# Moving the values' part, one VectorE sum and the last unit's products in a hand-ordered HGRN2 and MLP kernel

## The chip, the core and the metric

The kernel runs on one core of one Trainium2 chip. The metric is the device time of one execution in microseconds. TensorE, VectorE (DVE), ScalarE (ACT), GpSimd (POOL) and the queue of SyncE (SP) each work through a list of instructions of their own and wait for one another by semaphores.

## The reference

A gated linear attention with a state of 48 x 48 for each head is followed by a two-layer MLP with the quick GELU. All is float32.

```python
def _attn_ref(q, k, v, f_logit):            # (4, 8, 768, 48)
    f = 1.0 / (1.0 + np.exp(-f_logit))
    for t in range(S):
        state = f[:, :, t, :, None] * state + np.einsum('bhd,bhe->bhde', k[:, :, t], v[:, :, t])
        y[:, :, t] = np.einsum('bhd,bhde->bhe', q[:, :, t], state)

def _moe_ref(x, w_in, w_out):               # x: 3072 tokens x 384, d_ff 2048
    h = x @ w_in
    g = h * (1.0 / (1.0 + np.exp(-1.702 * h)))
    return g @ w_out
```

Between the two, y is brought from (batch, head, token, 48) to x with one row of 384 for each token.

## The kernel before

**Units and stages.** The 3072 tokens are cut into 12 units of 256. For each unit there is an attention part and an MLP part. The MLP of earlier units is used as filler: `fill` is a list of small jobs (columns of work, a function that emits them), and `merge(n, ...)` emits the attention of unit n part by part, each followed by so many jobs of `fill` as its share of the columns allows. For units 4 and up the shares are the numbers that `late(kind)` returns. TensorE and GpSimd keep the order in which the program emits their instructions. The orders of VectorE, ScalarE and SP are made by the scheduler of the framework from the same program.

**The attention of a late unit.** Its parts, in order, are: two parts "V" and one "V3", each of which makes the scores of two levels of a tree over the tokens (L406), multiplies the gates into X (`promote`, L492, VectorE), sets keys and queries aside (`set_aside`, L463 and L469, ScalarE) and masks the scores into A; "C" and "C2", in which the keys are transposed on VectorE, written to memory and fetched again (`carry_k` and `fetch_k`: L558, L563, L572), and copied to `kn` by ScalarE (L573); "B" and "B2", which transpose the gates and queries of the next unit; "S1", the values' part: `add` multiplies the values with A into the bank tile `y` (L503), and the keys `kn` with the values (L594), after which VectorE updates the state `st` (L609 to L613) and GpSimd multiplies gates together (`tot`, L397); "K3", the next keys. The products of the state with the queries (L634) are emitted with the first "V" of the next unit. Their result is copied to yT (L646), moved by DMA to xT (L669, L674), and summed to the operands E on GpSimd (`sums_of_x`, L879). In unit 11, the last, keys are turned on TensorE ("T"), and "S" and "W" close the attention.

**The MLP of a late unit.** h is made of 20 products of sums of w_in with sums of x instead of 24 (`mlp_h20`). An output out of 0 to 7 is a sum of several products, named in `PRODUCTS`: operands, the product on whose PSUM bank it goes on (its parent), and the outputs with signs.

```python
        ("c1", "q0", -1, ((0, -1),)), ("p1", "v", 2, ((6, -1),)), ("a21", "w", -1, ((5, -1),)), ("p3", "r3", 4, ((0, -1),)),
        ("c4", "w", 9, ((2, 1), (0, -1))), ("p9", "x", 7, ((1, -1),)), ("a20", "q0", 19, ((4, -1),)),
        ("p11", "y", 3, ((1, -1),)), ("p12", "b00", 10, ((2, 1),)), ("a30", "t", 18, ()), ("p14", "b01", 17, ((3, 1),)),
```

A product that goes on in its parent's bank must come after every reader of that bank; where a parent has two children, ScalarE copies the bank to another (L923). The first part of an output is copied to g by ScalarE (L935), the later ones are added by VectorE (L939), and when the last has come ScalarE takes the GELU in place (L941). c4 is the one product with two outputs: out 2 is copied from its bank, and its part of out 0 is then added from the copy in SBUF. The order of the products and the bank ("lane") of each stand in `WHOLE`; lanes 0 to 3 are four single banks, 4 and 5 the tile `y`, 6 and 7 the tile `sc`. The last unit has 258 columns and so does each product in two halves, of which the order is `HALVES` (a number of 20 and more is the second half). Then `sums_of_a` makes S from g (L720 to L724), and `mlp_o7` makes the output of 7 products of 8 matmuls each (L785), in the order Y, W, X, Y, Z, Y, Z, with `last_sum` (L729) after X; `lanes["o"]` gives their banks. In the last unit `sum_last` (L964, L966) sums one more token on VectorE.

Of the kernel before, what the change touches and what calls it, by code (L numbers as in the profile page):

```python
# [9 lines left out]
F32 = mybir.dt.float32  # L10
# [3 lines left out]
ALU = mybir.AluOpType  # L14
# [9 lines left out]
def kernel(  # L24
# [33 lines left out]
    nc = tc.nc  # L58
    B, H, S, D = q.shape
    DM = H * D  # L60
    DFF = moe_w_in.shape[1]
    P = 128
    C = 64
    G = 128
    U = 256
# [7 lines left out]
    NK = DM // P  # L73
# [15 lines left out]
    mlp = ctx.enter_context(tc.tile_pool(name="mlp", bufs=2))  # L89
# [13 lines left out]
    def bank(shape, name, lane=None):  # L103

        lane = next(turns) % 4 if lane is None else lane
        return ps.tile(shape, F32, tag=f"mm{lane}", name=name, bufs=1)
# [33 lines left out]
    at = [wp.tile([P, n], I32, tag="bits", name=f"at{j}", bufs=PAIRS_AHEAD) for j, n in enumerate((1, (NL - 1) * 64))]  # L140
# [35 lines left out]
    for r in range(NGR):  # L176
        ffs = range(r * FG, (r + 1) * FG)
        for ff in ffs[::2]:
            f = slice(ff * P, (ff + 2) * P)
# [132 lines left out]
    def attention(n):  # L312
# [304 lines left out]
        def _():  # L617
# [44 lines left out]
            if n > N_FILL:  # L662
                sums_of_x(n)
# [19 lines left out]
    HF, HC = NFF // 2, DM // 2  # L683
    T = {}
# [46 lines left out]
    def mlp_o7(n, g):  # L731
# [74 lines left out]
    WHOLE = tuple((x, 0, lane) for x, lane in (  # L806
        (18, 0), (0, 2), (7, 1), (2, 3), (17, 4), (15, 2), (9, 1), (13, 0), (19, 5), (1, 3),
        (14, 4), (4, 2), (10, 5), (6, 3), (8, 1), (3, 2), (5, 0), (16, 3), (12, 5), (11, 2),
    ))
    HALVES = tuple((x % 20, x // 20, lane) for x, lane in (  # L810
        (38, 7), (20, 1), (22, 2), (7, 0), (37, 7), (35, 1), (2, 6), (27, 3), (9, 0), (34, 5),
        (33, 4), (1, 6), (21, 2), (8, 0), (39, 7), (29, 3), (24, 4), (26, 2), (18, 5), (6, 6),
        (30, 7), (36, 2), (13, 0), (16, 6), (32, 7), (17, 5), (25, 1), (28, 3), (0, 7), (5, 2),
        (19, 6), (4, 0), (23, 4), (10, 6), (15, 7), (3, 0), (14, 5), (12, 6), (31, 4), (11, 0),
    ))
    lanes = {}
    WA = {f"a{i}{c}": w_in[:, c, ROW[i] * FG * P:(ROW[i] + 1) * FG * P] for i in range(ROWS) for c in range(NK)}
# [47 lines left out]
    def sums_of_x(n):  # L865

        w = (width(n) + 1) // 2
        sums = [mlp.tile([P, NK, width(n)], F32, tag="xT", name=f"E_{n}_{i}", bufs=3).rearrange("p c t -> p (c t)")
                for i in range(2)]
        at = iter([sums[i][:, j * w:(j + 1) * w] for i in range(2) for j in range(2 * NK)])  # L870
        e = E[n] = {f"b{c}{j}": xTs[n][:, c, j * w:(j + 1) * w] for c in range(NK) for j in range(2)}
        for out, x, op, y in (
            ("s7", "b11", "", "b21"), ("u", "b20", "", "b21"), ("z", "b01", "", "u"), ("q0", "z", "", "b00"),
            ("v", "u", "+", "b11"), ("w", "b10", "", "v"), ("t", "b01", "+", "b21"), ("x", "b00", "", "w"),
            ("q4", "q0", "+", "b10"), ("r3", "b00", "", "b10"), ("r3", "r3", "+", "b20"), ("y", "x", "", "b01"),
        ):
            if out not in e:
                e[out] = next(at)
            nc.gpsimd.tensor_tensor(e[out], e[x], e[y], ALU.add if op else ALU.subtract)  # L879
# [1 line left out]
    E = {}  # L881
    in_y = {}

    def mlp_h20(n, g):
        w = (width(n) + 1) // 2
        groups = 1 if FG * w <= 512 else 2
        wide = FG // groups
        plan = WHOLE if groups == 1 else HALVES
        lane_of = {(x, group): lane for x, group, lane in plan}
        left = {}  # L890
        for x, group, _ in plan:
            for out, _ in PRODUCTS[x][3]:
                left[out, group] = left.get((out, group), 0) + 1
        single = {key for key, times in left.items() if times == 1}
        begun, banks, shared = set(), {}, {}
        in_y[n] = len(plan)

        def take(lane, name):
            if lane < 4:
                banks[lane] = bank([P, wide, w], f"h_{n}_{name}", lanes["h"][lane])  # L900
            else:
                tag = "y" if lane < 6 else "sc"
                if tag not in shared:
                    shared[tag] = ps.tile([P, 2, 512], F32, tag=tag, name=f"h_{n}_{tag}")
                banks[lane] = shared[tag][:, lane % 2, :wide * w].rearrange("p (t x) -> p t x", x=w)
            return banks[lane]

        def product(x, group, lane):
            a, b, parent, parts = PRODUCTS[x]
            root = parent < 0  # L910
            ph = take(lane, f"{x}_{group}") if root else banks[lane]
            kids = [y for y in range(len(PRODUCTS)) if PRODUCTS[y][2] == x]
            goes_on = any(lane_of[y, group] == lane for y in kids)
            for t in range(wide):
                f = group * wide + t
                nc.tensor.matmul(  # L916
                    ph[:, t], lhsT=WA[a][:, f * P:(f + 1) * P], rhs=E[n][b], start=(root and t == 0), stop=not goes_on,
                    skip_group_check=True,
                )
            in_y[n] -= 1  # L920
            for y in kids:
                if lane_of[y, group] != lane:
                    nc.scalar.copy(take(lane_of[y, group], f"{y}_{group}"), ph)  # L923
            part, turned = ph, 1
            for out, sign in parts:
                key = out, group
                f = ROW[out // 2] * FG + group * wide
                to = g[f // HF][:, f % HF:f % HF + wide, out % 2 * w:(out % 2 + 1) * w]
                left[key] -= 1
                if key in single:  # L930
                    nc.scalar.activation(to, ph, AF.Gelu_apprx_sigmoid, scale=float(sign))
                    continue
                if key not in begun:
                    begun.add(key)
                    nc.scalar.activation(to, ph, AF.Copy, scale=float(sign))  # L935

                    part, turned = to, sign
                    continue
                nc.vector.tensor_tensor(to, to, part, ALU.add if sign == turned else ALU.subtract)  # L939
                if not left[key]:  # L940
                    nc.scalar.activation(to, to, AF.Gelu_apprx_sigmoid)  # L941

        def begin():
            for half in range(2):
                g[half] = g_tile(f"g_{n}_{half}", width(n))
            free = lanes["o"]

            lanes["h"] = [free[x] for x in (1, 2, 0, 3)]
            lanes["o"] = [lanes["h"][x] for x in (1, 0, 3, 2)]

        def end():
            sums_of_a(n, g)
            if width(n) > U:
                sum_last(g)

        return [(0, begin, 0)] + [(wide * w, lambda x=x: product(*x), 0) for x in plan] + [(0, end, 0)]

    def sum_last(g):

# [12 lines left out]
    def width(n):  # L972

        return U + 2 * (n == NALL - 1)

    def g_tile(name, w=U):
        return mlp.tile([P, HF, w], F32, tag="g", name=name, bufs=3)
# [39 lines left out]
        for lo, hi in ((1, 113), (113, P)) if r0 < 0 else ((0, P),):  # L1017
            nc.sync.dma_start(out=out[r0 + lo:r0 + hi, :], in_=o[lo:hi])

    def mlp_unit(n):  # L1020
        g = {}

        def last_token():
            po = ps.tile([P, DM], F32, tag="sc", name="o_last")
            nc.tensor.matmul(po[:1], lhsT=ones, rhs=g["last"][:, 0], start=True, stop=True)
            nc.scalar.copy(g["last"][:1, 0], po[:1])
            nc.sync.dma_start(out=out[NALL * U - 1:, :], in_=g["last"][:1, 0])
        o = mlp_o7(n, g)
        if width(n) > U:
            o.insert(6 * HF, (DM, last_token, 0))  # L1030
        if n > N_FILL:
            return mlp_h20(n, g) + o
        by_block = {}

        def end():

            g[0], g[1] = (by_block["tile", i] for i in range(2))
            sums_of_a(n, g)
            sums_in_place(nc.gpsimd)
            lanes["o"] = [next(turns) % 4 for _ in range(4)]  # L1040
        return mlp_h(n, range(NFF), by_block) + [(0, end, 0)] + o[:HF] + [(0, lambda: sums_in_place(nc.vector), 0)] + o[HF:]

    sums = {}
# [113 lines left out]

    def late(kind):

        return {"V": 7, "V3": 3, "C": 2, "C2": 4, "S1": 3, "S": 7, "B": 3, "B2": 4, "K3": 3, "T": 2, "W": 5}.get(kind, 0)  # L1160

    UNIT = NFF * NK * U + U // P * NFF * DM
    H20 = 20 * FG * G
# [16 lines left out]
    fill = []  # L1180
# [7 lines left out]
    merge(3, fill, 3 * UNIT // 2 - LAG // 2, steady, 7, by=0.7, chores=w_sums, per=1)  # L1188
    fill_order.close()
    for n in range(N_FILL, NALL):  # L1190
        fill += mlp_unit(n)
    with nc.allow_non_contiguous_dma("one token"):
        for h in range(2):
            nc.sync.dma_start(out=q_end[h * HS:h * HS + D], in_=q[B - 1, h::2, S - 1, :].rearrange("a d -> d a"))
# [6 lines left out]
    for n in range(4, NALL):  # L1201
        merge(n, fill, (H20 if n > N_FILL + 1 else NFF * NK * U) + 7 * HF * HC, late, chores=w_sums if n == 4 else [])
# [31 lines left out]
```

## Time and profile before

| what | before |
| --- | --- |
| median of 3 runs (lowest to highest) | 626.68 us (626.68 to 627.51) |
| the profiled execution: time, span | 629.15 us, 627.4 us |
| mean granted TensorE clock | 0.989 |
| TensorE matmuls, 7824 | 586.6 us busy (93%) |
| TensorE weight loads | 519.4 us (83%) |
| VectorE, ScalarE, GpSimd | 433.3 us (69%), 293.0 us (47%), 135.8 us (22%) |
| chain of work that ended last: TensorE, VectorE, ScalarE, DMA | 68%, 15%, 7%, 4% |
| start of L594 in units 5 to 10 | 285.95, 331.85, 377.53, 423.45, 469.17, 514.21 us |
| last unit: first product of h, first matmul of o, end | 579.94, 602.99, 627.4 us |

A row of the trace gives the start in us from the beginning of the span, the duration, the engine (PE matmul, PEld weight load, DVE, ACT, POOL, SPq for a DMA issue), the line and the tiles; "x16" says that 16 instructions stand in one row; one float32 matmul shows as two. In brackets stands how long the engine had been idle and what released it.

### The profile page before, as it was taken

The numbers are of one execution on the slowest core, as the hardware profiler recorded it, in microseconds if no ns is written. First come the engines' busy times: TensorE is split into PE (matmuls) and PEld (weight loads), VectorE is DVE, ScalarE is ACT, GpSimd is POOL, SyncE is SP. The second block draws the span as 40 slices with busy tenths as digits, with TensorE's granted clock in tenths as the row PEclk, the third lists the DMA queues.
The fourth block names the chain that finished last, engine by engine and source line by source line (L and its number), as shares of the span: only waits on it lengthen the run. The fifth ranks groups of instructions, "written<-read, shape, count | busy, mean of one in ns | idle before, by whom it ended". The sixth has DMA issues, their size and how long they took to land.

```text
span 627.4 us, 18499 instructions
## 1 busy us (share of the span) xinstructions
PE 586.6 (93%) x7824; PEld 519.4 (83%) x7824; DVE 433.3 (69%) x693; ACT 293.0 (47%) x611; POOL 135.8 (22%) x215
## 2 busy tenths in 40 slices
PE   6869899889999999999999999989989999999896
PEld 5656776657768689898998999989989989989886
DVE  1799966665887677689577689677687685461293
ACT  3466633343325354365365374474464464542530
POOL 3020200230035405501502501502502404203000
PEclk9979999979999999999999999999999999999999
DMA  7746756741044543433543243443251111001000
GB/s 172 203 121 168 186 137 168 167 125 51 2 104 94 139 114 78 107 83 102 138 105 74 72 111 73 126 124 76 74 150 40 44 53 27 26 2 39 14 1 27
DMA packets 83317, 58.31 MB, mean 93 GB/s; under 512 B 33634, under 2 KB 75266, under 8 KB 83234
## 3 DMA queue, kind: packets, MB, share of 16 engines
q1 hardware_dynamic: 82480, 55.94, 35.7%
q10 hardware_dynamic: 753, 1.18, 0.8%
q8 instruction: 62, 1.02, 0.7%
q14 instruction: 22, 0.17, 0.1%
HBM read 43.98 MB, written 8.39 MB: 83 GB/s over the span
## 4 chain that ended last, share of the span: by engine, by line
PE 68%; DVE 15%; ACT 7%; DMA 4%; issue 3%; SPq 1%; POOL 1%; DVEq 0%; ACTq 0%; POOLq 0%
PE h L916 11%; PE o_Y L785 10%; PE h L993 9%; PE o L1007 8%; PE o_Z L785 7%; PE sc L406 6%; PE h_y L916 4%; PE o_X L785 4%; PE o_W L785 3%; DVE g L939 2%; ACT g L941 2%; ACT kn L573 2%; PE t L350 2%; PE y L634 1%; PE sc L594 1%
## 5 line engine op out<-in xcount | busy, mean ns | idle before, releaser
L492 DVE TENSOR_TENSOR X<-X,tot 128x1024 f32<-128x1024 f32 x45 | 57.7, 1282 | 65.2 <-PE sc L406 55.2
L993 PE MATMUL h<-xT,w_in 128*128 128x256 f32 x384 | 89.3, 388 | 1.1 <-issue 0.7
L463 ACT COPY Kc<-X 128x512 f32<-128x512 f32 x72 | 48.1, 668 | 86.6 <-DVE X L492 59.7
L993 PEld LDWEIGHTS h<-xT,w_in 128*128 128x128 f32 x384 | 73.0, 193 | 13.2 <-issue 1.1
L1007 PE MATMUL o<-w_out,g 128*128 128x384 f32 x192 | 68.1, 504 | 2.4 <-DVE w_out L228 2.0
L397 POOL TENSOR_TENSOR tot<-F 128x512 f32<-128x512 f32 x12 | 12.5, 1040 | 245.3 <-DVE st L612 239.1
L916 PE MATMUL h<-E,w_in 128*128 128x128 f32 (+1 forms) x428 | 56.8, 277 | 3.2 <-DVE g L939 3.2
L1007 PEld LDWEIGHTS o<-w_out,g 128*128 128x128 f32 x192 | 36.5, 195 | 25.9 <-DVE w_out L228 2.6
L916 PEld LDWEIGHTS h<-E,w_in 128*128 128x128 f32 x428 | 51.7, 192 | 4.3 <-issue 3.9
L785 PE MATMUL o_Y<-T,S 128*128 128x192 f32 x288 | 51.7, 329 | 1.1 <-ACT osb L759 1.1
L941 ACT ACTIVATE g<-g 128x512 f32<-128x512 f32 (+1 forms) x63 | 35.9, 584 | 28.2 <-DVE g L939 28.0
L997 ACT ACTIVATE g<-h 128x256 f32<-128x256 f32 x64 | 24.0, 382 | 52.9 <-PE h L993 52.5
L785 PEld LDWEIGHTS o_Y<-T,S 128*128 128x128 f32 x288 | 47.1, 190 | 1.9 <-ACT osb L759 1.4
L456 DVE COPY_PREDICATED A<-masks,sc 128x256 f32<-128x256 uint32 x96 | 42.2, 510 | 0.0
L646 ACT COPY yT<-y 48x256 f32<-48x256 f32 x96 | 35.1, 365 | 11.0 <-PE y L634 9.8
L406 PE MATMUL sc<-X,Kc 48*64 48x64 f32 x1440 | 31.4, 224 | 7.8 <-DVE A L435 3.4
L406 PEld LDWEIGHTS sc<-X,Kc 48*64 48x64 f32 x1440 | 26.6, 138 | 14.5 <-ACT Kc L463 7.8
L338 DVE STREAM_TRANSPOSE X<-raw 128x512 f32<-128x512 f32 x36 | 38.1, 1106 | 0.2
L939 DVE TENSOR_TENSOR g<-g,h 128x512 f32<-128x512 f32 (+1 forms) x49 | 31.5, 647 | 8.3 <-PE h L916 7.2
L935 ACT ACTIVATE g<-h 128x512 f32<-128x512 f32 (+1 forms) x52 | 28.0, 554 | 17.0 <-PE h L916 16.0
L365 POOL TENSOR_SCALAR F<-F 128x1024 f32<-128x1024 f32 x11 | 13.4, 1217 | 102.1 <-ACT F L368 79.1
L879 POOL TENSOR_TENSOR E<-xT 128x128 f32<-128x128 f32 (+1 forms) x32 | 19.0, 603 | 69.9 <-DMA xT<-yT 42.1
(150 smaller groups left out, 1163.2 us busy)
## 6 DMA issues: line engine op xcount, KB each, us to landing
bits<-in_moe_w_out_dram SPq DMA_DIRECT2D x8, 768.0 KB, 8.0
raw<-in_f_logit_dram SPq DMA_DIRECT2D x48, 96.0 KB, 2.4
raw<-in_k_dram SPq DMA_DIRECT2D x48, 96.0 KB, 2.3
raw<-in_q_dram SPq DMA_DIRECT2D x44, 96.0 KB, 2.3
bits<-in_moe_w_in_dram SPq DMA_DIRECT2D x7, 576.0 KB
k_tok<-z SPq DMA_DIRECT2D x56, 64.0 KB, 1.7
kt<-k_tok SPq DMA_DIRECT2D x14, 256.0 KB, 2.8
xT<-yT SPq DMA_DIRECT2D x24, 144.0 KB, 2.7
```

What stands on the lines that cost most here:

```text
L338: nc.vector.transpose(view(out, at, [[HALF, NP], [step, R4], [R4 * step, 32]]), by_half[:, j, f].rearrange("p a (j d) -> p (a j) d", j=R4) ...
L406: nc.tensor.matmul(t["sc"][g * HS:(g + 1) * HS, h, a, s, :], lhsT=t["Kc", l][rows(h), x:x + HS], rhs=rhs(h, a, g), start=True, stop=True,)
L456: nc.vector.copy_predicated(out=view(A, at, dims), mask=mask.bitcast(U32), data=got)
L463: nc.scalar.copy(c.rearrange("p (n two m) -> p n two m", two=2, m=m), view(X, KF * SLOT, [[2 * m, SLOT // (2 * m)], [(KR - KF) * SLOT + m, ...
L492: nc.vector.tensor_tensor(x, x, y, ALU.mult)
L646: nc.scalar.copy(view(yT[rows(h)], at, [[U, NP], [step, HS]]), py[columns(h, g), g, :, f, :])
L785: nc.tensor.matmul(t[name], lhsT=lhs(f), rhs=rhs(f), start=(new and i == 0), stop=(i == HF - 1), skip_group_check=True,)
L916: nc.tensor.matmul(ph[:, t], lhsT=WA[a][:, f * P:(f + 1) * P], rhs=E[n][b], start=(root and t == 0), stop=not goes_on, skip_group_check=True,)
L939: nc.vector.tensor_tensor(to, to, part, ALU.add if sign == turned else ALU.subtract)
L941: nc.scalar.activation(to, to, AF.Gelu_apprx_sigmoid)
L993: nc.tensor.matmul(ph, lhsT=w_in[:, c, ff * P:(ff + 1) * P], rhs=xTs[n][:, c, :], start=(c == 0), stop=(c == NK - 1))
L1007: nc.tensor.matmul(t["po"], lhsT=g[ff // FG][:, ff % FG, tt * P:(tt + 1) * P], rhs=w_out[:, ff, :], start=(ff == ffs[0]), stop=(ff == ffs[ ...
```

## The change

Five edits, none of which adds or removes a matmul, a sum or a transfer.

1. `late` has new shares: V 6 for 7, S1 2 for 3, B 4 for 3, B2 5 for 4, K3 2 for 3. In the built program of each of units 5 to 10 the second scores come 2 o matmuls earlier, the third scores 2 products earlier, and L503 and L594 come 6 o matmuls later (after 8 of Y instead of 2). In unit 11 L634 comes after 4 matmuls of Y instead of 6.
2. In `mlp_h20` a part of an output that lies in SBUF is put off until the next part of that output has been added from its bank.
3. `HALVES` has another order and other lanes, and four marks (-1, -1).
4. The last 16 jobs of `fill`, the last two products of o of unit 10, are taken out of it and emitted in fours at the marks, among the first five half products of unit 11.
5. `sums_of_x` of the last unit makes the sums in another order: t, the seventh, comes fifth; y comes last as before, x ahead of it.

GpSimd's four sums of w_in in unit 4 come ahead of the gates' products (L397) as a result of edit 1.

```diff
+    HALVES = tuple((x % 20 if x >= 0 else None, x // 20, lane) for x, lane in (
+        (38, 1), (-1, -1), (0, 6), (37, 4), (-1, -1), (-1, -1), (39, 4), (-1, -1), (34, 5), (2, 7),
+        (15, 6), (30, 4), (33, 1), (22, 0), (18, 3), (1, 7), (20, 2), (25, 5), (32, 4), (24, 1),
+        (6, 7), (35, 2), (13, 6), (17, 3), (21, 0), (23, 1), (16, 7), (4, 5), (7, 2), (19, 4),
+        (26, 0), (27, 7), (5, 6), (14, 3), (10, 4), (9, 2), (29, 7), (3, 5), (36, 0), (31, 1),
+        (12, 4), (8, 2), (28, 7), (11, 5),
     ))
...
+        if width(n) > U:
+            sums = [sums[i] for i in (0, 1, 2, 3, 6, 4, 5, 8, 9, 10, 7, 11)]
...
-                nc.vector.tensor_tensor(to, to, part, ALU.add if sign == turned else ALU.subtract)
+                if part is not ph and left[key]:
+                    later[key] = part, sign * turned
+                    continue
+                for part, sign in ((part, sign * turned), *filter(None, [later.pop(key, None)])):
+                    nc.vector.tensor_tensor(to, to, part, ALU.add if sign > 0 else ALU.subtract)
...
-        return [(0, begin, 0)] + [(wide * w, lambda x=x: product(*x), 0) for x in plan] + [(0, end, 0)]
+        items = [(0, begin, 0)]
+        for x in order:
+            if x[0] is None:
+                items += before[:4]
+                del before[:4]
+            else:
+                items.append((wide * w, lambda x=x: product(*x), 0))
+        assert not before
+        return items + [(0, end, 0)]
...
+        if width(n) > U:
+            before = fill[-2 * HF:]
+            del fill[-2 * HF:]
...
-        return {"V": 7, "V3": 3, "C": 2, "C2": 4, "S1": 3, "S": 7, "B": 3, "B2": 4, "K3": 3, "T": 2, "W": 5}.get(kind, 0)
+        return {"V": 6, "V3": 3, "C": 2, "C2": 4, "S1": 2, "S": 7, "B": 4, "B2": 5, "K3": 2, "T": 2, "W": 5}.get(kind, 0)
```

## The prediction

> **What bounds the kernel now.** I read the busy table first, then the waits, then two stretches by time. TensorE's order is written out by hand, so every wait of TensorE moves all that stands behind it. The summary line and the waits of its weight loads (columns: us in total, times, longest):
>
> ```profile
> PE 586.6 (93%) x7824; PEld 519.4 (83%) x7824; DVE 433.3 (69%) x693; ACT 293.0 (47%) x611; POOL 135.8 (22%) x215
> ```
>
> ```profile
> PEld sc L594 <- ACT kn L573: 7.3, 7, 1.3
> ...
> PEld h L916 <- issue: 3.9, 4, 1.4
> ...
> PEld y L503 <- DVE g L939: 3.5, 5, 1.4
> ```
>
> No other engine is near full, yet TensorE waits in each late unit for two things: the turned keys `kn`, and a PSUM bank that VectorE has not yet read. By time, the end of the products in the stage of unit 9 (columns: start, us, engine, line; idle before and its releaser in brackets):
>
> ```profile
> 463.56 0.69 DVE L939 TENSOR_TENSOR g<-g 128x512 f32<-128x512 f32 x1 [0.79 <-ACT g L935]
> 464.36 0.69 DVE L939 TENSOR_TENSOR g<-g,h 128x512 f32<-128x512 f32 x1
> ...
> 465.19 1.13 PE L916 MATMUL h<-E,w_in 128*128 128x128 f32 x8 [0.66 <-DVE g L939]
> ...
> 466.16 0.82 PE L785 MATMUL o_Y<-w_out,g 128*128 128x192 f32 x4
> ...
> 466.28 1.83 ACT L941 ACTIVATE g<-g 128x512 f32<-128x512 f32 x3 [0.57 <-DVE g L939]
> ...
> 466.90 1.11 PE L503 MATMUL y<-A,vt 64*48 64x64 f32 x64
> ...
> 468.01 1.10 ACT L573 COPY kn<-kt 128x512 f32<-128x512 f32 x1
> ...
> 469.17 1.03 PE L594 MATMUL sc<-vt,kn 64*64 64x48 f32 x56 [1.15 <-ACT kn L573]
> ```
>
> The reader is to see two stalls. The sum `g<-g` reads SBUF only, waits for ScalarE, and stands in front of the sum that frees the bank of p3; product p11 on that bank comes late. Then `kn` is copied behind three GELUs, and the values' products (L594) wait for it, since two o matmuls alone stand between the products and the values' part. In units 6 and 8 the first stall falls on L503 instead (1.4 us: it needs the bank of p12). The last stage, by busy time (us; busy of PE, PEld, DVE, ACT, POOL), and one of its waits:
>
> ```profile
> 580.00:603.00 23.00, 20.15 (x162) 18.55 (x161) 9.34 (x23) 12.62 (x34) 0.00 (x0) 1.00 0.03 10
> ...
> 584.44 0.61 PE L916 MATMUL h_y<-xT,w_in 128*128 128x129 f32 x4
> 585.16 0.42 DVE L939 TENSOR_TENSOR g<-g,h_y 128x258 f32<-128x258 f32 x1 [4.50 <-PE h_y L916]
> ...
> 585.64 0.52 PEld L916 LDWEIGHTS h_y<-E,w_in 128*128 128x128 f32 x4 [0.78 <-DVE g L939]
> ```
>
> Here each of the 40 half products waits for its bank's last reader: eight waits in a stage in which no engine is full.
>
> **What the Trainium skill says.** "Perfetto Trace Analysis", section Identifying the Most-Contended Engine: matmul busy time is a poor measure of headroom, weight-load busy a better one. The trace agrees: in the last stage PE shows 20.15 of 23.00 us, though a half product with no wait starts every 0.445 us (586.08, 586.52, 586.97), so 40 need 17.8. The same page, Optimization Strategy, advises interleaving stages with different limits; no run yet shows what that is worth here. Its section Optimizing Tensor Performance has independent matmul groups rotate over banks so that evacuations overlap: the old order returns to a bank after as little as three to four products. "PSUM — Partial Sum Buffer", section Engine vs sequencer instructions: the queues of ScalarE, VectorE and GpSimd are strict FIFO. The trace agrees: the second kt transfer is issued at 462.24, lands 2.8 us later, and its copy runs at 468.01, behind the GELUs.
>
> **The change part by part.** No matmul, sum or transfer is added or removed; all five edits move work. Where they move it I took from the order of the built programs.
>
> *1. Pacing (`late`).* In the stages of units 5 to 10 the values' part (L503, L594) comes after eight o_Y matmuls instead of two: 6 x 0.328 us (o_W: 2.60 us for 8) = 1.97 us more cover. Removed wait: `kn`, 7 x about 1.0 = 7.3 us. TensorE would come to L594 at 466.90 + 1.0 + 1.97 = 469.9 in unit 9, against `kn` ready at 469.1; ScalarE's order also puts that copy ahead of one or two GELUs in most units. The same cover takes the two 1.4 us waits of L503, 2.8. If it failed, `kn` would have to be 1.97 us later than now. Of L503's five waits I leave the three of 0.23.
>
> *2. The SBUF sum behind the bank's sum.* p3's sum no longer waits for ScalarE: it can start when VectorE is free at 462.8 instead of 464.36, so p11 loses its wait: 3.9 us over four stages. In even units VectorE has an attention product (L492) ahead of that sum; I leave 0.2 us three times, 0.6. Bounds for edits 1 and 2 together: 9 to 14.0 us gained.
>
> *3. What is late next.* With six o matmuls fewer behind L594, the chain of the attention shows: states (8 x 0.39), `tot` on GpSimd (1.04), F's transposes (2.06), tanh, the yT copies (3.01), Kc, L492, Kc, then the second scores. From the end of L594 to the second Kc is ready it now takes 13.6 us (470.24 to 483.8; even: 424.53 to 438.3), of which 0.25 to 0.7 is VectorE finishing the sums of g, which will be done earlier: 13.1 to 13.3. TensorE's own way to the second scores will be 12 o (3.93) + L634 (0.93) + the first scores (1.2) + 20 o (6.55) = 12.6 us. Now it is 15.4, which leaves the margin seen here:
>
> ```profile
> 483.17 0.62 ACT L463 COPY Kc<-X 128x512 f32<-128x512 f32 x1 [1.07 <-DVE X L492]
> ...
> 485.61 0.69 PE L406 MATMUL sc<-Qc,Kc 48*64 48x64 f32 x32
> ```
>
> So a new wait of 0.5 to 0.9 us; I take 0.7 in six units, 4.2 us. (At unit 4 a like wait, 1.4 us on o_Y after L844, is there already and I leave it.) Bounds: 0 (if the chain loses its VectorE part and the 0.6 us shuffle of values) to 1.5 each, 9 us. The third scores come 1.8 us earlier among the products, but from the second scores to the fourth Kc copy it takes 6.1 us and TensorE has 7.3 of work: covered. L634 follows L594 by 3.93 us, the states need 3.2: covered by 0.7.
>
> *4. Queues passed.* DVE, ACT and SP are in a scheduler's order: a shuffle of values (0.58) moves ahead of L492 in one unit, the key transposes move ahead of sums of g, vr and raw loads change places on SP. SP is idle from 470.8 to 479.2 in unit 9, so I cost these at nothing; without that gap an xT transfer would be up to 4 us late, against E sums that are ready some 4 us before their use. In unit 4 four GpSimd sums of w_in (about 1.26 each) move ahead of the gates' products; GpSimd is idle there until 241.87, so nothing.
>
> *5. Unit 11.* Four o_Y instead of two stand behind L634, which waits for the states in any case: 2 x 0.33 = 0.7 us lost.
>
> *6. The last h.* 16 o matmuls of unit 10 (5.2 us) now stand in four groups among the first five half products, the least return to a bank rises from 1.3-1.8 us to 2.2 us, and a bank's turn takes 0.72 (matmul to reader) + 0.42 + 0.06 = 1.2 us plus queueing. Stage now: 579.94 to 602.99 = 23.05 us, needed 17.8, so 5.2 is lost; I take 4.8 as regained. The E sums on GpSimd are the risk of the earlier start: by the rows of now s7 (first) is done at 574.5, q0 (fourth) at 575.9 and t, now fifth, at 576.4; with edit 5 the products that read them come at about 575.6, 577.3 and 577.8. Bounds 2 to 5.2. VectorE's end work (sum_last 15 x 0.62) ends at 616.2, 2.6 us before it is read at 618.80: it covers one or two of those sums being later.
>
> Sum: -7.3 - 2.8 - 3.9 + 0.6 + 4.2 + 0.7 - 4.8 = **-13.3 us**. On the profiled execution that is 627.4 to 614.1 of span (its own time 629.15). The median of the runs shown, 626.68, lies 2.5 below that time, so I subtract from the median: **613.4**.
>
> **Rivals.** (a) *No new wait*: the attention chain shortens as much as TensorE's way. For it: VectorE starts the states later than it must today. Against: GpSimd, ScalarE and VectorE rows of it are fixed. -13.3 - 4.2 = -17.5: 609. (b) *The cover is half spent*: the second scores wait 1.5 us in six units (+4.8) and the last stage keeps 2 us more of its waits: -6.5: 620. For it: ScalarE and VectorE queue in bursts (three GELUs in a row). (c) *Slower*: the second scores (L406) become the bound of every late unit. Without that wait the change gains 17.5, so it turns slower where the wait exceeds 17.5 / 6 = 2.9 us, a chain of 15.5 us or more after L594; at 3.5 us the sum is +3.5: 630. Against: the longest now is 13.8. (d) *It doesn't do what it says*: the moves cover waits that come back at the next product, and the time stays at 626 to 627. Against: the order of TensorE does change in every late unit and the waits have 1.97 us to hide 1.3.
>
> **How the numbers follow.** Forecast 0.60 (610 to 617), (a) 0.12, (b) 0.17, (c) 0.07, (d) 0.04. The range 607.5 to 621 takes in the forecast, (a) and (b). A measurement can tell 0.2%, 1.3 us, from no change. Faster 0.89, same 0.04, slower 0.07.
>
> **What would show it.** Right: L594's wait for `kn` is gone or under 0.3; p11 and L503 show no wait for g beyond 0.2; a wait L406 <- Kc or X of 0.5 to 0.9 stands before the second scores; from the first last-unit product to the first o_Y of that unit 23 to 24 us pass with the 16 o matmuls inside. Wrong: a wait over 1.5 us at L406, L634 or an early half product, or late units still 45.7 to 45.9 us apart (I expect 44.1).

## The result, and the profile after

The changed kernel takes 622.95 us (median of 20 runs, 619.80 to 627.41) against 626.87 us before (20 runs, 625.47 to 630.63): the ratio of the means is 0.9947, 95% interval 0.9926 to 0.9967, and the medians lie 3.9 us apart. The forecast was 13.3 us less. The profiled execution has a time of 625.44 us, a span of 623.5 us and a mean clock of 0.985.

The waits of TensorE's weight loads in the late units, 238 to 552 us of the changed kernel (total, times, longest):

```profile
PEld sc L406 <- ACT osb L762: 9.6, 6, 2.9
PEld h_y L922 <- DVE g L950: 2.0, 5, 0.6
...
PEld y L503 <- DVE S L720: 0.9, 4, 0.2
PEld y L503 <- DVE g L722: 0.5, 2, 0.2
```

The wait for `kn` at L594 (7.3 us before), the wait of p11 (3.9) and the long waits of L503 are gone, as forecast. In their place stand 9.6 us at L406, the second scores. The end of the products in the stage of unit 9, by time:

```profile
462.20 0.68 DVE L950 TENSOR_TENSOR g<-g,h 128x512 f32<-128x512 f32 x1
...
462.83 2.77 PE L785 MATMUL o_Y<-w_out,g 128*128 128x192 f32 x16
...
463.45 1.13 ACT L573 COPY kn<-kt 128x512 f32<-128x512 f32 x1
...
465.52 1.11 PE L503 MATMUL y<-A,vt 64*48 64x64 f32 x64
...
466.46 1.10 PE L594 MATMUL sc<-vt,kn 64*64 64x48 f32 x64
```

Eight o matmuls now cover the copy of `kn`, which is done at 464.58, 1.9 us before it is used. So edits 1 and 2 do what they say. Fifteen microseconds later come the second scores of the next unit, unit 10:

```profile
477.56 2.76 PE L785 MATMUL o_Z<-T,g 128*128 128x192 f32 x16
...
480.04 1.29 DVE L456 COPY_PREDICATED A<-masks,sc 128x256 f32<-128x256 uint32 x2
480.15 0.62 ACT L463 COPY Kc<-X 128x512 f32<-128x512 f32 x1 [1.08 <-DVE X L492]
...
481.44 0.59 PEld L406 LDWEIGHTS sc<-Qc,Kc 48*64 48x64 f32 x32 [1.41 <-ACT osb L762]
481.47 0.70 PE L406 MATMUL sc<-Qc,Kc 48*64 48x64 f32 x32 [1.15 <-DVE A L456]
```

The second scores start at 481.47. Kc is ready at 480.77, but L456, with which VectorE reads the first scores out of the tile `sc`, ends at 481.33. The weight load's row names an older ScalarE copy, the matmul's row names the one that ended last. The last stage, from the first half product to the first o_Y, with the 16 o matmuls in it, and its waits:

```profile
573.48:600.98 27.50, 24.92 (x194) 23.59 (x194) 9.79 (x24) 11.95 (x33) 1.06 (x3) 1.00 0.04 16
```

```profile
PEld h_sc L922 <- DVE g L950: 1.1, 1, 1.1
PEld h_sc L922 <- ACT g L941: 0.9, 2, 0.7
PEld h_y L922 <- ACT g L937: 0.7, 1, 0.7
PEld h_sc L922 <- ACT h_sc L929: 0.6, 1, 0.6
PEld h_y L922 <- DVE g L950: 0.6, 2, 0.3
```

Before, 23.05 us and 5.2 us for the same o matmuls make 28.25. So 0.75 us was gained where 4.8 was forecast: seven waits, 3.9 us together, are left, all of them on lanes 4 to 7. And the clock: stretches of 2.5 us of the changed kernel after the new wait of unit 5, and after L634 in unit 11 (busy time of PE, PEld, DVE, ACT and POOL, then the granted clock, DMA share and GB/s):

```profile
252.50:255.00 2.50, 0.66 (x5) 0.37 (x3) 1.77 (x3) 1.43 (x4) 0.00 (x0) 1.00 0.42 96
255.00:257.50 2.50, 1.69 (x67) 1.66 (x68) 1.06 (x3) 0.55 (x3) 1.66 (x4) 0.95 0.64 160
257.50:260.00 2.50, 2.50 (x10) 2.50 (x9) 2.50 (x6) 1.14 (x2) 2.42 (x5) 0.50 0.66 134
260.00:262.50 2.50, 2.50 (x15) 2.50 (x14) 1.71 (x3) 0.62 (x1) 2.42 (x5) 0.87 0.20 37
...
555.00:557.50 2.50, 1.14 (x43) 0.79 (x45) 2.33 (x7) 0.00 (x0) 0.00 (x0) 1.00 0.00 0
557.50:560.00 2.50, 2.50 (x47) 2.35 (x48) 0.59 (x2) 1.52 (x5) 0.00 (x0) 0.53 0.02 7
560.00:562.50 2.50, 2.50 (x10) 2.50 (x9) 0.00 (x0) 2.03 (x7) 0.00 (x0) 0.50 0.33 70
562.50:565.00 2.50, 2.50 (x11) 2.50 (x10) 0.00 (x0) 0.00 (x0) 0.00 (x0) 0.61 0.40 87
```

By the clock record of the trace, of which these are means, the clock stands at half for 3.4 us in unit 5 and for 6.8 us in unit 11, and matmuls there take up to nearly twice as long: in unit 11, 4 matmuls of o_Y and 8 of o_W together take 2.75 us more than elsewhere. Before, the clock at the same place of unit 11 stayed full:

```profile
560.00:562.50 2.50, 1.78 (x45) 1.19 (x47) 2.33 (x7) 0.00 (x0) 0.00 (x0) 1.00 0.00 0
562.50:565.00 2.50, 2.28 (x52) 2.15 (x53) 0.61 (x2) 1.76 (x5) 0.00 (x0) 1.00 0.02 7
```

Adding up the profiled executions: from L594 of unit 4 to L594 of unit 11 the kernel gained 4.9 us (319.21 to 314.32), forecast 9.2. From there to the start of the last o_Z it lost 2.9 (62.11 to 65.00), forecast a gain of 4.1. What is left of the 3.9 us of span is the last store, which took 4.6 us from its issue to the end before and 2.8 after and has nothing to do with the change.

### The profile page after: what moved, and what is told of

Read it like the earlier page. It is cut to its first block, busy times and chain, and to the rows that moved or that the text cites. A ratio compares the mean times of both kernels' runs of the same rounds, so it can differ in the third digit from the quotient of the medians.

```text
span 623.5 us, 18501 instructions
## 1 busy us (share of the span) xinstructions
PE 586.5 (94%) x7824; PEld 521.3 (84%) x7824; DVE 434.4 (70%) x693; ACT 291.5 (47%) x611; POOL 138.4 (22%) x215
## 4 chain that ended last, share of the span: by engine, by line
PE 61%; DVE 18%; ACT 8%; issue 5%; DMA 4%; SPq 2%; POOL 1%; DVEq 0%; ACTq 0%; POOLq 0%
PE h L922 13%; PE h L1012 9%; PE o_Y L785 8%; PE o L1026 6%; PE h_y L922 5%; PE o_Z L785 5%; PE sc L406 5%; ACT yT L646 4%; DVE g L950 2%; PE t L350 2%; DVE X L492 2%; DVE A L456 2%; PE o_W L785 2%; DVE F L338 2%; PE o_X L785 1%
## 5 line engine op out<-in xcount | busy, mean ns | idle before, releaser
L1026 PE MATMUL o<-w_out,g 128*128 128x384 f32 x192 | 66.0, 492 | 2.1 <-DVE w_out L228 1.7
L397 POOL TENSOR_TENSOR tot<-F 128x512 f32<-128x512 f32 x12 | 12.5, 1041 | 215.5 <-DVE st L612 209.6
L922 PE MATMUL h<-E,w_in 128*128 128x128 f32 (+1 forms) x420 | 53.4, 275 | 0.0
L922 PEld LDWEIGHTS h<-E,w_in 128*128 128x128 f32 x420 | 50.1, 192 | 0.0
L785 PEld LDWEIGHTS o_Y<-T,S 128*128 128x128 f32 x288 | 48.5, 195 | 0.5
L950 DVE TENSOR_TENSOR g<-g,h 128x512 f32<-128x512 f32 (+1 forms) x52 | 32.8, 632 | 15.4 <-PE h L922 10.3
L456 DVE COPY_PREDICATED A<-masks,sc 128x256 f32<-128x256 uint32 x96 | 42.2, 509 | 0.0
L406 PE MATMUL sc<-X,Kc 48*64 48x64 f32 x1440 | 30.8, 221 | 8.7 <-DVE A L435 3.5
L406 PEld LDWEIGHTS sc<-X,Kc 48*64 48x64 f32 x1440 | 26.1, 134 | 15.4 <-ACT Kc L463 7.9
L941 ACT ACTIVATE g<-h 128x512 f32<-128x512 f32 (+1 forms) x46 | 26.1, 577 | 16.7 <-PE h L922 16.5
L950 DVE TENSOR_TENSOR g<-g,h_y 128x512 f32<-128x512 f32 (+1 forms) x26 | 16.4, 632 | 21.9 <-PE h_y L922 21.7
```

The costliest lines, as they stand in the source:

```text
L406: nc.tensor.matmul(t["sc"][g * HS:(g + 1) * HS, h, a, s, :], lhsT=t["Kc", l][rows(h), x:x + HS], rhs=rhs(h, a, g), start=True, stop=True,)
L456: nc.vector.copy_predicated(out=view(A, at, dims), mask=mask.bitcast(U32), data=got)
L785: nc.tensor.matmul(t[name], lhsT=lhs(f), rhs=rhs(f), start=(new and i == 0), stop=(i == HF - 1), skip_group_check=True,)
L922: nc.tensor.matmul(ph[:, t], lhsT=WA[a][:, f * P:(f + 1) * P], rhs=E[n][b], start=(root and t == 0), stop=not goes_on, skip_group_check=True,)
L950: nc.vector.tensor_tensor(to, to, part, ALU.add if sign > 0 else ALU.subtract)
L1026: nc.tensor.matmul(t["po"], lhsT=g[ff // FG][:, ff % FG, tt * P:(tt + 1) * P], rhs=w_out[:, ff, :], start=(ff == ffs[0]), stop=(ff == ffs[ ...
```

## The experiments

Three theories were to be told apart for where some 9 us went. *Bank*: the second scores wait for the bank pair `sc`, not for Kc. *Shared tile*: lanes 4 and 5 (tile `y`) and 6 and 7 (tile `sc`) wait for each other's readers, so that the returns to a bank that the forecast counted lane by lane come at half the distance. *Clock*: new idle spots let the clock fall. Against them stand three rivals: Kc sets the wait, as was forecast; the readers of each lane are late by themselves; the dips of the clock come by chance. Each run is compared with runs of the kernel before on the same chip, whose medians lay between 626.57 and 627.46 us. Where the clock matters, the span times the mean clock is given too: the time that a run would have taken, as an estimate, had no clock been lost.

**One edit at a time.** The kernel before, with the new shares of `late` alone:

```diff
-        return {"V": 7, "V3": 3, "C": 2, "C2": 4, "S1": 3, "S": 7, "B": 3, "B2": 4, "K3": 3, "T": 2, "W": 5}.get(kind, 0)
+        return {"V": 6, "V3": 3, "C": 2, "C2": 4, "S1": 2, "S": 7, "B": 4, "B2": 5, "K3": 2, "T": 2, "W": 5}.get(kind, 0)
```

> The kernel before with the new shares of late() alone. Theory of the bank: the waits for kn and the two long ones of L503 are gone (10 us less), but the second scores of each late unit now wait 1.1 to 1.5 us (2.9 in unit 5) until VectorE has copied the first scores out of their PSUM tile (L456), some 9 us more, and unit 11 loses 0.7: 626 to 627 us, no change. Theory of the forecast (the second scores wait for Kc alone, 0.7 us): 5 us less, 621.5.

Measured: 627.71 us, ratio 0.9992 (0.9977 to 1.0007). Its waits:

```profile
PEld sc L406 <- ACT osb L762: 8.9, 6, 2.9
...
PEld h L916 <- issue: 2.0, 4, 0.6
```

The wait at L406 takes back most of what the wait for `kn` (7.3 us) and those of L503 (2.1) gave, and p11 still waits 2.0 us of its 3.9. The time stays the same only together with the clock: span times mean clock is 615.2 us on average for 618.9 before (38 runs), and the mean clock fell from 0.989 to 0.9835. The new order of half products alone (edits 3 to 5):

```diff
-    HALVES = ...    # the old order
+    HALVES = ...    # the new order with its four marks
+            before = fill[-2 * HF:]
+            del fill[-2 * HF:]
```

> The kernel before with the last unit's new order, its marks and the new order of its sums of x alone. Theory of the coupled tile: two lanes that share a PSUM tile (4 and 5, 6 and 7) wait for each other's readers, so the last stage keeps 4 us of waits and takes 27.5 us with the 16 o matmuls inside, 0.6 us less than now: 626 us. Theory of the forecast (each lane waits for its own readers): 23 to 24 us, 4.8 us less: 622.

Measured: 626.58 us, ratio 0.9985 (0.9970 to 0.9999). The stage runs from 575.23 to 602.78, 27.55 us, with the same seven waits as in the changed kernel. The sum put off, alone (edit 2):

```diff
+                if part is not ph and left[key]:
+                    later[key] = part, sign * turned
+                    continue
```

> The kernel before with only the SBUF sum put behind the bank's sum. If kn, whose copy stands behind GELUs of those sums, comes earlier with them, the four waits of p11 (3.9 us) go and 623 is reached. If kn stays where it is, L594 waits longer by as much as p11 waits less, and the time stays at 626 to 627.

Measured: 634.79 us, ratio 1.0081 (1.0047 to 1.0116), with these waits:

```profile
PEld sc L594 <- ACT kn L573: 10.2, 7, 2.1
...
PEld y L503 <- DVE g L944: 5.6, 6, 1.4
```

What p11 no longer waits (3.9 us before) comes back, and somewhat more, at L594 (10.2 for 7.3) and L503 (5.6 for 3.5): 5.0 us. Alone, edit 2 gains nothing, since TensorE only arrives earlier at a wait whose end is fixed. The added time, which was not expected, is clock: span times mean clock is 619.2 us on average, 618.9 before. Three runs at a mean clock of 0.976 took 634.6 to 636.4 us, and the one at 0.989 took 627.57. The profiled one shows dips near 380, 475 and 570 us.

**The bank of the scores.** The second scores of units 5 to 11 go into the tile `y`, which nobody uses at that time:

```diff
-        def scores():
-            t["sc"] = ps.tile([P, 2, NP, 2, HS], F32, tag="sc", name=f"sc_{n}_{next(serial)}")
+        def scores(tag="sc"):
+            t["sc"] = ps.tile([P, 2, NP, 2, HS], F32, tag=tag, name=f"sc_{n}_{next(serial)}")
...
-            scores()
+            scores("y" if l == 2 and n > N_FILL + 1 else "sc")
```

> The changed kernel with the second scores of units 5 to 11 written into the tile y (free since the yT copies) instead of the tile of the first scores. Theory of the bank: their wait falls from 1.1 to 1.5 us to the 0.5 to 0.9 that Kc needs, about 5 us less than the changed kernel: 618. If Kc or another engine's work bounds them, the waits stay at 1.1 to 1.5 and the time at 623.

Measured: 617.80 us, ratio 0.9841 (0.9821 to 0.9860). In this kernel some products of h replace the parent that was copied into their bank of `y` instead of adding to it; number and kind of the instructions are the same. The Trainium skill, "PSUM — Partial Sum Buffer", section The four PSUM rules, says why: a matmul with a start mark (a flag that begins a new sum) clears the accumulate bits of its whole bank in the partitions it writes, and a later matmul without one overwrites where the bit is clear. With the mark on the first matmul of each bank and half of the partitions alone, the products add again, which agrees with the page:

```diff
+            tag = "y" if n > N_FILL + 1 and l in (2, 3) else "sc"
...
-                        start=True, stop=True,
+                        start=tag == "sc" or (s == 0 and a == 0), stop=True, skip_group_check=True,
```

> The changed kernel, with the second scores of units 5 to 11 put into the bank pair of y instead of sc, as in the earlier run, and a start mark only on the first matmul of each bank and partition half. Bank theory (the second scores waited for VectorE to read the first ones out of sc): the L406 wait of 9.6 us stays away, time 617 to 618.5. Clock theory (only the short dips at half clock make the difference): 620 to 623. Forecast theory (the chain of the copies Kc sets the wait): the wait comes back as a wait for Kc of 0.5 to 0.9 in six units, time 622 to 623.

Measured: 614.83 us, ratio 0.9799 (0.9770 to 0.9827): 8 us less than the changed kernel, more than expected. On average 6.5 us of it are shorter waits (span times mean clock 606.1 us for 612.6) and 2.0 are clock. The second scores of unit 10 again, and those of unit 5:

```profile
474.96 1.32 DVE L457 COPY_PREDICATED A<-masks,sc 128x256 f32<-128x256 uint32 x2
475.08 0.62 ACT L464 COPY Kc<-X 128x512 f32<-128x512 f32 x1 [1.07 <-DVE X L493]
475.15 0.56 PEld L407 LDWEIGHTS sc<-Qc,Kc 48*64 48x64 f32 x32 [0.23 <-issue]
475.15 0.69 PE L407 MATMUL sc<-Qc,Kc 48*64 48x64 f32 x32
...
253.42 0.56 PEld L407 LDWEIGHTS sc<-Qc,Kc 48*64 48x64 f32 x32 [0.39 <-ACT Qc L470]
255.33 0.56 PEld L407 LDWEIGHTS sc<-X,Kc 48*64 48x64 f32 x32 [1.35 <-ACT Kc L464]
```

In unit 10 they start while VectorE is still reading the first ones (L457 here is L456 there), and do not wait for the second Kc either: the first half of them needs the first Kc alone, and the second half starts 0.46 to 0.68 us after the first in units 6 to 10, so the second Kc costs at most some 0.2 us there. Unit 5 is the exception: with the bank free, its second scores still wait 0.39 us for Qc and 1.35 for the second Kc, so that of the 2.9 us in the changed kernel some 1.2 were the bank's. L594 is now 43.55 to 43.96 us apart in the middle units (44.56 to 45.05 in the changed kernel; forecast 44.1). The bank theory holds in units 6 to 10, and in unit 5 for the lesser part of the wait.

**The shared tiles.** `y` as two tiles of one bank, everything else as changed:

```diff
-                tag = "y" if lane < 6 else "sc"
+                tag = f"y{lane - 4}" if lane < 6 else "sc"
...
-            t["py"] = ps.tile([P, NG, NP, 2, HS], F32, tag="y", name=f"y_{n}")
+            t["py"] = [ps.tile([P, NP, 2, HS], F32, tag=f"y{g}", name=f"y_{n}_{g}") for g in range(NG)]
```

> The changed kernel, with the two-bank tile y split into two tiles of one bank each, so that lanes 4 and 5 of the h products no longer share a tile; lanes 6 and 7 still share sc. Shared-tile theory: the waits of (32,4), (19,4), (3,5) in the last stage (1.3 us) and the five waits h_y <- g in the stages of units 5 to 9 (2.0 us) go, those on lanes 6 and 7 stay; time 619.5 to 621.5. Queue theory (the readers on ScalarE and VectorE are simply late, each lane for itself): the waits stay where they are and the time stays at 622 to 624.

Measured: 619.35 us, ratio 0.9870 (0.9850 to 0.9890). All its waits in the last stage:

```profile
PEld h_sc L922 <- DVE g L950: 1.1, 1, 1.1
PEld h_sc L922 <- ACT g L941: 0.9, 2, 0.7
PEld h_sc L922 <- ACT h_sc L929: 0.7, 1, 0.7
```

The waits on h_y are gone (1.3 us), those on h_sc, whose tile is still shared, stand within 0.1 us, and the stage takes 26.1 us. The five h_y waits of the earlier stages (2.0 us) are gone too; in turn L406 waits 10.6 us for 9.6. The order of products and the readers are the same, so it is the tile that couples lanes 4 and 5, and not late readers. The tile `sc` was not split; that it couples lanes 6 and 7 alike is inferred, and the orders below rest on it.

Then the order of half products was searched again with a count per tile: 0.445 us for a product, 0.80 from its start to its reader, and the readers in order on ScalarE and VectorE. The first such order, in the changed kernel and together with the second scores in `y`:

> The changed kernel, with another order and other lanes for the 40 half products of the last unit, found by counting returns per PSUM tile (lanes 4 and 5 together, 6 and 7 together) with 0.445 us per product and 0.80 us to a reader plus the queues of ScalarE and VectorE. The same count gives 27.2 us for the changed kernel's last stage with its 16 o matmuls (measured 27.5) and 22.9 for the kernel before (measured 23.05 without them). Shared-tile theory: no wait in the last stage, 23.0 to 23.7 us from the first half product to the first o_Y, time 618.5 to 620. Supply theory (sums of E on GpSimd, or the GELUs of g behind the last product, take the place of the waits): stage 26 us or o_Y late, time 621.5 to 623.

> Second scores in y (with the marks as above) and the new order of half products together. If the two misses are independent: 617.8 - 3.6 = 614.2, range 613 to 616. If the last stage's gain is lost to something the earlier arrival uncovers: 616.5 to 618.

Measured: 620.41 us, ratio 0.9898 (0.9871 to 0.9924), and 613.17 us, ratio 0.9770 (0.9750 to 0.9789). In both, products of the last unit replace a copied parent instead of adding to it; in this order three of the single banks, lanes 1 to 3, start with a copy. The instructions are as before. No half product waits, but o_Y waits 1.5 us: the wait moved to the stage's end. The next order starts each lane outside the tile `y` with a product that has no parent, as the order before the change did:

> Second scores in y, and an order of half products counted per tile as in f3/f4, in which the first product on each lane is one that has no parent and in which the GELUs that the first o_Y reads come earlier. Count for the last stage: 23.4 us with the 16 o matmuls (one wait of 0.37). Shared-tile theory: the stage takes 23.3 to 23.8 us, o_Y follows without its wait of 1.5 us, time 611 to 613. If the wait before o_Y only moves to the next o product: 613 to 614.

> The changed kernel with that order of half products alone. Shared-tile theory: 23.3 to 23.8 us for the last stage in place of 27.5, so 622.9 - 3.9 = 619.0, range 618 to 620.5. Supply theory: 621.5 or more.

Measured: 615.71 us, ratio 0.9809 (0.9789 to 0.9828), and 622.32 us, ratio 0.9913 (0.9891 to 0.9935): no clear gain over the kernels without it, a miss. The stage is shorter, 25.05 us in both for 27.5, but two terms were not in the count. The first product of the new order waits for a sum of E on GpSimd (0.2 us in f5, 1.8 in f6), and the last half product lies on lane 1, the bank that o_Y takes next, so that o_Y waits 1.44 us for VectorE. In f6 the two take back most of the gain; why f5 isn't faster than f1, whose trace is 1.6 us longer, stays open. With both counted:

```diff
+        (38, 0), (-1, -1), (33, 4), (-1, -1), (-1, -1), (22, 2), (25, 4), (0, 6), (20, 1), (-1, -1),
+        (35, 1), (24, 5), (15, 6), (37, 0), (2, 3), (18, 7), (21, 2), (34, 0), (1, 3), (13, 7),
+        (17, 4), (39, 1), (6, 3), (4, 6), (26, 2), (16, 3), (19, 4), (14, 0), (30, 1), (27, 3),
+        (23, 5), (5, 7), (7, 0), (29, 3), (10, 4), (9, 0), (31, 5), (36, 2), (3, 6), (32, 1),
+        (12, 4), (8, 0), (28, 3), (11, 6),
```

> Second scores in y, and an order of half products counted per tile that also counts when each sum of E is ready and leaves the bank of the first o_Y (lane 1) free five products before the end. In f5 these two cost 0.2 us (sum of E) and 1.44 us (o_Y waited for VectorE to read its bank). Shared-tile theory with these two terms: last stage 23.4 us with the 16 o matmuls, o_Y at once, time 1.6 us under f5's 615.7 at the same clock: 612.5 to 614.5. If the stage is bound elsewhere: 615 to 616.

Measured: 612.67 us, ratio 0.9786 (0.9756 to 0.9816). Its last stage by busy time:

```profile
561.95:585.48 23.53, 23.21 (x192) 23.05 (x192) 9.84 (x24) 11.57 (x32) 3.70 (x9) 1.00 0.05 18
```

and all that its weight loads wait in that stretch:

```profile
PEld h_y L923 <- issue: 0.5, 1, 0.5
```

23.5 us to the first weight load of o_Y, 23.6 to its first matmul, against a count of 23.4, where the changed kernel needs 27.5. It is the best version tried that computes what the kernel computes. Against f1 its time alone does not decide, as the intervals of the two ratios overlap; the stage's own length does.

**The clock.** Matmuls that nobody reads, put into two waits:

```diff
+            if n == 5 and l == 2:        # g1: N_FILL + 1, which is unit 4
+                keep_up(4, into=ps.tile([P, 2, 512], F32, tag="y", name="idle_y")[:, 0, :(NL - 1) * 64])
...
+            if n == NALL - 1:
+                keep_up(2, into=bank([P, (NL - 1) * 64], "idle_z", lanes["o"][3]))
```

> The changed kernel with matmuls that nobody reads put into two waits of TensorE: four (128x320) ahead of the second scores of unit 5, two ahead of L634 in unit 11. Activity theory (the clock falls to half after a stretch in which TensorE did little): the dips near 257 and 560 us are gone or rarer, mean clock over the runs up from 0.985 to about 0.989, time 2 us less, about 621. Chance theory (the dips come at these places or others whatever TensorE does): mean clock and time stay as they are, 622 to 624. If the added matmuls cost more than the waits hold: 623.5 to 625.

Measured: 624.28 us, ratio 0.9948 (0.9931 to 0.9965), mean clock 0.9885 over six runs. The four matmuls stood at 207.6 us, outside the wait, and cost their 2.3 us, so its time decides nothing. Its trace shows one thing: in unit 5 TensorE was idle for 2.65 us, uncovered, and the clock stayed full. In the right place:

> The changed kernel with matmuls that nobody reads inside two waits of TensorE: four (128x320, 0.43 us for each half) ahead of the second scores of unit 5, whose wait is 2.9 us, and two ahead of L634 in unit 11, whose wait is 1.1 us. In g1 the four stood in unit 4 by mistake and cost their 2.3 us. Activity theory (half clock follows a stretch in which TensorE did little): the dips at 255 to 262 and 557 to 565 us stay away, mean clock 0.988 to 0.990 over the runs (0.985 without), time 620.5 to 621.5. Chance theory: mean clock 0.985, time 622 to 624.

Measured: 620.58 us, ratio 0.9907 (0.9883 to 0.9931), mean clock 0.9898. The start marks of the added matmuls make products of one unit replace copied parents, as in e4. The stretches after unit 5's wait:

```profile
252.50:255.00 2.50, 2.35 (x10) 1.37 (x8) 2.23 (x3) 1.43 (x5) 0.00 (x0) 1.00 0.38 85
255.00:257.50 2.50, 2.15 (x70) 2.12 (x71) 1.07 (x2) 0.08 (x1) 2.13 (x4) 1.00 0.68 177
257.50:260.00 2.50, 2.50 (x18) 2.50 (x17) 2.50 (x6) 1.14 (x2) 2.42 (x5) 1.00 0.57 110
```

TensorE is busy 2.35 of 2.5 us where it was busy 0.66, and the clock stays full; the dip in unit 11 is gone as well. All six runs have a clock of 0.989 or more, against 7 of the 20 of the changed kernel. Span times mean clock is nearly the same (613.0 and 612.6 us), so the 2.4 us are clock alone. The numbers favour the activity theory, though the two ratios' intervals overlap and g1's trace shows that a spot makes a dip likely, not certain.

## Why the prediction was wrong in size

**Right.** The direction, and edits 1 and 2: the waits for `kn`, of p11 and the long ones of L503 go, and what is late next is the second scores. The sign of being wrong that the prediction named, over 1.5 us at L406, came: 2.9 in unit 5 and 1.53 in unit 7. In unit 11, L634 waits 1.07 us instead of 0.43, the 0.7 of step 5. The moves on the other queues (step 4) cost nothing that the trace shows.

**Step 3 failed: what ends the wait at L406.** I took Kc, ready at 483.79 in what I called unit 9 (these second scores are unit 10's), as the end of the chain, with TensorE's start at 485.61 as its margin. This row of the trace of before, 0.12 us ahead of the Kc row that I showed, ends later:

```profile
483.05 1.30 DVE L456 COPY_PREDICATED A<-masks,sc 128x256 f32<-128x256 uint32 x2
```

It ends at 484.35 and frees the only buffer of `sc`. The margin was 1.26 us, not 1.82, and with TensorE 2.8 us earlier and the chain up to 0.7 earlier it had to end as a wait of 0.8 to 1.5; 1.12 to 1.53 was measured in units 6 to 10 and 2.9 in unit 5, where the 1.4 us that I left standing at o_Y went into it. So 9.6 us in place of 5.6 (4.2 + 1.4). The Kc wait of 0.7 did not exist in units 6 to 10, as f1 shows: the first half of the second scores doesn't read the second Kc. In unit 5 f1 leaves 1.35 us of it. Rival (b) named the size, 1.5 us in six units, and not the cause.

**Step 6 failed: what of the last stage is regained.** 4.8 us was taken, 0.75 measured (27.50 for 28.25). The prediction's count took each lane as a bank of its own and found no return under 2.2 us. Lanes 4 and 5, and 6 and 7, lie in one tile each, and a product waits for the last reader of either. The h_y wait of 0.78 that I showed from the trace of before was one of these, lane 4 behind the reader of lane 5, and could have told me. With the order counted by tile the 4 us came (f7).

**A term that was not in the sum: the clock.** Over the runs the changed kernel loses 9.1 us to clock below full (20 runs) and the one before 6.9 (38 runs; span times one less the mean clock, averaged): 2.2 us. By span times mean clock the change gained 6.3 us. Two spots are the likely cause, the 2.9 us wait of step 3 and unit 11's shorter cover of step 5, at which TensorE does little for some microseconds. With both covered, in g2, 6.3 us of clock are lost in place of 9.1.

Smaller ones: p11's 0.6 in even units became h_y waits of 2.0 us (0.6 before), from tile `y` again, and L503 kept 1.4 us in six short waits where I had left 0.7; the short issue gaps at L406, 1.2 us, went into the longer wait. The three misses of 4.0, 4.05 and 2.2 add up to 10.3, where 9.4 us lie between forecast and result; the smaller terms nearly cancel. Two further edits, the scores' bank and the order by tile, bring the kernel to 612.67 us. That this is near the forecast of 613.4 is chance: it took edits that the forecast did not have.

## What to carry to other kernels

Ask of a TensorE instruction not only when its operands are ready but also when the tile that it writes is free, and take the later: a second buffer (here an idle tile) was worth 8 us, 6.5 of them without the clock, where more cover had for the most part moved the wait. Count returns to a bank in the unit by which waits are set, here the tile and not the bank, and let the count reproduce the waits of the old trace before trusting it with a new order. A gain early in a hand-ordered queue is worth what the next fixed end leaves of it: the sum put off gained nothing alone.

## What was not expected of the hardware

A wait of 2 to 3 us can cost nearly as much again in clock. In unit 5 TensorE was busy 0.66 of 2.5 us and then the clock stood at 0.50 for 3.4 us; 8 matmuls of o_Y took 4.4 us instead of 2.6. The clock records show a grid: in every trace of this case a half-clock stretch that the end of the run does not cut off lasts 3.41 us or two or three times that, and within one trace the starts lie whole multiples of 3.41 us apart. In the changed kernel they are at 42.22, 257.25 and 557.63 us, 63 and 88 steps. The Trainium skill, "TensorE: Matmul & The Clock Gate", section HAM oscillation, tells of matmuls that start at half clock after a gap of over some 3.4 us, and its Part 1 tells of a window that runs free of the kernel. The value of one half agrees, and the grid fits such a window. The gap here was shorter (2.6 us, with small matmuls after it), and a like gap of 2.65 us in g1 had no dip, which fits too: it may depend on how a gap lies on the grid. How little work in a step brings the dip is not shown. The runs of one kernel, over 7 us apart, group by clock: for the changed kernel 619.80 us at 0.992 and 626.76 to 627.41 at 0.977 to 0.978.
